# Inverse transforms in the FFN's PSUM ring next to forward ones, one place per step for convolution work, gated stores of kept spectra, and more heat matmuls

## The chip, the cores and the metric

The program runs on one core of one Trainium2 chip. The metric is the device time of one launch in microseconds, the median of several runs. Clocks: TensorE (PE) runs at one of two levels, 1.2 or 2.4 GHz; the profile gives the granted share, where 1.00 is 2.4 GHz and 0.50 is 1.2 GHz.

## What is computed

A long convolution, gated by x, is followed by a feed-forward network (FFN) on every token. Everything is float32 in and out.

```python
# x, v: [4, 12480, 128]; pos_emb: [12480, 64]; w_in: [128, 2048]; w_out: [2048, 128]
h_filt = (np.maximum(pos_emb @ w1, 0) @ w2) * np.exp(-0.01 * pos)[:, None]
y = irfft(rfft(x * v, 2 * S) * rfft(h_filt, 2 * S))[:, :S]
t = (x * y).reshape(49920, 128)
h = t @ w_in
out = (h * sigmoid(1.702 * h)) @ w_out
```

## The kernel before

The FFT is written as matmuls. A sequence half of 6240 points is split as 52 x 120, and the work is cut into five sets `o` (0 to 4): set 0 is the first half of batch 0 and of the filter, set 1 the first half of batch 1 and the filter's second half, set 2 the first halves of batches 2 and 3, sets 3 and 4 the second halves of all four. Each set passes three stages.

- **Stage p1** (`p1_start` for set 0, `p1_unit` for the others): transforms of 120 points, 26 units of a set; results go to DRAM (`g_d`).
- **Stage p2** (`p2_start` for set 0, `p2_unit` for the others): 31 units of a set. A unit loads its piece of `g_d`; `forward` (L315) makes the transform of 52 points, four float32 matmuls of 52 rows by 64 columns that sit on the four quarters of the array and write two PSUM banks; VectorE multiplies the spectra; `inverse` (L321), four matmuls of the same shape, goes back into two banks, which ScalarE copies out to `z`; a DMA writes `z_d`. In the trace each of these float32 matmuls is two records, so that a block of four is "x8".
- **Stage p3** (`p3_unit`): the last inverse step, sixteen records on L508, then the product with x, split into a high and a low part `xh`, `xl` for the FFN.

The FFN works on 104 "halves" of 480 tokens, eight steps each, 832 steps in all. A step is `mm1` (six matmuls of 480 columns into one of two tiles `h`, each two banks), two GELU passes on ScalarE (`fgh` rounded, `fg` full), one subtraction on VectorE (`fgl`, by `lo`), and three steps later `mm2` (six matmuls into `acc`). The first PSUM pool of this phase, tag `cv`, has three banks for all of the convolution; the tag `h` has two tiles of two banks; `acc` has one.

The order is by hand, in a fixed program order for each engine. At first set 0 passes p1 and p2 alone (the start phase), with `heat(k)`: 2k matmuls of zeros, 256 columns of bf16, whose results nobody reads. A short prologue computes `p3_unit(0)`. Then the 832 steps run, and the other sets' p1 and p2 units are fed in between: `feed.run(0.5)` stands at two places in a step, one after `mm1` and one after `mm2`, and lets as many pieces (up to a `yield`) of the units be written as the pace of that set asks for. `pipe` moves all live units on by one piece when a new one begins, so that a unit's inverse comes two units after its forward. All p2 units of sets 3 and 4 multiply two old spectra too (L410 to L424), so that they have more VectorE work.

24 of set 0's spectra are kept in SBUF until the FFN runs. They are stored by 48 DMAs that are written at steps 1 and 9 on GpSimd's queue (L706); the room that they leave is the later units' pool.

Names and lines that matter below: `forward` L318, `inverse` L324, `mm1` L581, `mm2` L598, GELU L582 and L583, `lo` L589, p3's matmuls L508, heat L655, the spectra's stores L375 and L376, p3's loads L482, L486 and L488, and the loads `pt` L193 and matmuls L198 with which set 1 begins.

## Time and profile before

| | us |
|---|---|
| median of 3 runs | 3064.37 (3063.86 to 3067.53) |
| the profiled execution | 3067.85 |
| its span, first to last instruction | 3066.1 |
| PE busy in the span | 3007.3 |
| VectorE (DVE) busy | 2153.9 |
| ScalarE (ACT) busy | 2068.8 |

The median is the number to beat; the profile is of one execution, whose span leaves out 1.75 us around the program. A busy PE is not a PE at its peak: matmuls overlap each other, their ends are modelled, and a record's length is longer than the distance to the next record. So the cost of a piece of PE work is read from the distance between starts, or from what a stretch holds beside a known number of steps.

### The profile page before, as it was taken

The page shows a single profiled execution, that of the slowest core. Times are in us where ns is not written, and L with a number is a line of the kernel's source. Part 1 is how long each engine was busy: PE and PEld are TensorE (multiplying, and loading weights), DVE is VectorE, ACT ScalarE, POOL GpSimd, SP SyncE. Part 2 cuts the span into 40 slices and gives each one's busy share as a digit, 9 for nine tenths or more (in the row PEclk, how much of TensorE's full clock was granted, in tenths as well). Part 3 has the DMA queues.
Part 4 walks back from the last instruction along what each step waited for, and adds up shares of the span by engine and source line. Part 5 has one row for each costly group of instructions (what it writes and reads, how often), then busy time and mean ns, then how long its engine had stood idle before and what let it go on. Part 6 is the DMA issues. An engine that isn't in the chain of part 4 may idle for free.

```text
span 3066.1 us, 42511 instructions
## 1 busy us (share of the span) xinstructions
PE 3007.3 (98%) x15368; PEld 2319.2 (76%) x15368; DVE 2153.9 (70%) x2909; ACT 2068.8 (67%) x2813; POOL 469.9 (15%) x764
## 2 busy tenths in 40 slices
PE   8889999999999999999999999999999999999999
PEld 4348876688666788777768887777778888888888
DVE  6656777777777667999996469898885444454444
ACT  3447766687777777666667766666667677767676
POOL 2363111022100111101111111011111111111110
PEclk9889999999999999999999999999999999999999
DMA  9889998899777966656665334454541111111110
GB/s 286 280 297 264 256 282 269 272 313 306 252 257 259 299 193 192 202 186 202 190 188 168 107 94 153 160 166 159 170 148 63 48 59 45 54 52 45 60 45 27
DMA packets 261105, 541.87 MB, mean 177 GB/s; under 512 B 30978, under 2 KB 120762, under 8 KB 260898
## 3 DMA queue, kind: packets, MB, share of 16 engines
q1 hardware_dynamic: 205970, 377.29, 39.0%
q0 software_dynamic: 54928, 161.86, 17.5%
q8 instruction: 124, 2.03, 0.3%
q14 instruction: 83, 0.68, 0.1%
HBM read 330.24 MB, written 208.80 MB: 176 GB/s over the span
## 4 chain that ended last, share of the span: by engine, by line
PE 63%; issue 27%; DVE 4%; POOL 3%; DMA 3%; ACT 1%; SPq 0%; POOLq 0%; ACTq 0%; DVEq 0%
PE acc L598 22%; PE h L581 22%; PE cv L318 4%; PE cv L508 4%; PE cv L324 4%; PE cv L178 1%; PE cv L179 1%; PE cv L180 1%; POOL zt L482 1%; PE cv L258 1%; DMA vt<-in_c_v_dram 1%; PE wb L655 1%; DVE fgl L589 1%; POOL out_dram L609 1%; POOL x L488 1%
## 5 line engine op out<-in xcount | busy, mean ns | idle before, releaser
L589 DVE TENSOR_TENSOR fgl<-fg,fgh 128x960 fp32r<-128x960 f32 x832 | 960.1, 1156 | 604.9 <-ACT fg L583 540.7
L582 ACT ACTIVATE fgh<-h 128x960 fp32r<-128x960 f32 x832 | 810.3, 974 | 574.3 <-PE h L581 573.6
L581 PE MATMUL h<-xh,wi 128*128 128x480 f32 x3328 | 1132.2, 384 | 1.3 <-ACT fg L583 1.2
L598 PE MATMUL acc<-fgh,wo 128*128 128x480 f32 x3328 | 884.2, 387 | 0.0
L583 ACT ACTIVATE fg<-h 128x960 f32<-128x960 f32 x832 | 807.3, 970 | 24.1 <-DVE fgl L589 24.0
L581 PEld LDWEIGHTS h<-xh,wi 128*128 128x128 f32 x3328 | 626.0, 188 | 188.7 <-issue 71.5
L598 PEld LDWEIGHTS acc<-fgh,wo 128*128 128x128 f32 x3328 | 610.2, 188 | 169.7 <-issue 81.7
L581 PE MATMUL h<-xl,wi 128*128 128x480 f32 x1664 | 632.2, 380 | 0.2 <-DVE xl L527 0.2
L598 PE MATMUL acc<-fgl,wo 128*128 128x480 f32 x1664 | 500.5, 382 | 1.7 <-DVE fgl L589 1.7
L609 POOL DMA_DIRECT2D out_dram<-ot x104 | 57.1, 549 | 2001.9 <-ACT ot L602 1999.9
L598 PEld LDWEIGHTS acc<-fgl,wo 128*128 128x128 f32 x1664 | 312.9, 188 | 51.5 <-DVE fgl L589 2.1
L581 PEld LDWEIGHTS h<-xl,wi 128*128 128x128 f32 x1664 | 312.8, 188 | 47.3 <-DVE xl L527 0.5
L508 PEld LDWEIGHTS cv<-vt,zt 122*128 122x128 f32 x1664 | 203.6, 194 | 29.1 <-issue 10.5
L508 PE MATMUL cv<-vt,zt 122*128 122x120 f32 x1664 | 206.6, 278 | 12.0 <-DMA vt<-in_c_v_dram 12.0
L318 PE MATMUL cv<-g,wf 52*64 52x512 f32 (+1 forms) x1240 | 186.0, 640 | 13.4 <-DVE t L355 5.7
L482 POOL DMA_DIRECT2D zt<-z_d x204 | 148.4, 733 | 14.9 <-issue 8.7
L466 ACT ACTIVATE z<-cv 128x512 f32<-128x512 f32 (+2 forms) x248 | 120.4, 544 | 43.0 <-PE cv L324 42.8
L324 PE MATMUL cv<-t,wv 52*64 52x512 f32 (+2 forms) x992 | 129.2, 555 | 5.4 <-DVE e L446 4.0
L311 ACT ACTIVATE a<-cv 128x512 f32<-128x512 f32 x208 | 119.0, 609 | 16.2 <-PE cv L180 15.3
L518 DVE TENSOR_TENSOR a<-cv,yq 128x240 f32<-128x240 f32 (+1 forms) x101 | 40.8, 404 | 119.8 <-ACT yq L516 119.6
L278 POOL DMA_DIRECT2D ft<-in_c_f_dram x108 | 57.6, 535 | 423.8 <-PE cv L180 420.1
L602 ACT ACTIVATE ot<-acc 128x480 f32<-128x480 f32 x104 | 59.5, 572 | 86.1 <-PE acc L598 86.1
(89 smaller groups left out, 2537.8 us busy)
## 6 DMA issues: line engine op xcount, KB each, us to landing
g_d<-a SPq DMA_DIRECT2D x260, 256.0 KB
g<-g_d SPq DMA_DIRECT2D x300, 208.0 KB
zt<-z_d POOLq DMA_DIRECT2D x204, 256.0 KB, 4.3
e<-e_d SPq DMA_DIRECT2D x180, 256.0 KB
z_d<-z SPq DMA_DIRECT2D x90, 512.0 KB
xt<-in_xv_dram SPq DMA_DIRECT2D x78, 480.0 KB
u<-us_d SPq DMA_DIRECT2D x60, 512.0 KB
ft<-in_c_f_dram POOLq DMA_DIRECT2D x108, 240.0 KB, 4.6
```

Of the source, the lines that this page charges most:

```text
L311: act(a[:, ri], b, ACTF.Copy)
L318: mm(out=xy[q ^ c][64 * c:64 * c + 64, 0:256 * nw].rearrange("p (w c) -> p w c", w=nw), lhsT=wf[64 * q:64 * q + N2, c], rhs=g[64 * q:64 * ...
L324: mm(out=ab[h][64 * pl:64 * pl + 64, 0:w].rearrange("p (w c) -> p w c", w=nw), lhsT=wv[64 * h:64 * h + N2, pl], rhs=y[pl ^ h][64 * h:64 * ...
L466: act(zv[:, :, h], ab[h][:, 0:wd].rearrange("p (w c) -> p w c", w=nw), ACTF.Copy)
L482: q.dma_start(out=zv[:, gq], in_=z_d[o][64 * gq + 2 * p0:64 * gq + 2 * p0 + 2 * npr].rearrange("r k c -> k r c"))
L508: mm(out=b[:, c0:c0 + M], lhsT=lhs, rhs=rhs, start=(k == 0), stop=(k == 1))
L581: mm(out=h[:, i, 0:TW], lhsT=wt[:, s], rhs=xx, start=st, stop=sp)
L582: act(gh, h[:, :, 0:TW], ACTF.Gelu_apprx_sigmoid)
L583: act(gf, h[:, :, 0:TW], ACTF.Gelu_apprx_sigmoid)
L589: tt(out=gl, in0=gf, in1=gh.bitcast(F32), op=ALU.subtract)
L598: mm(out=acc, lhsT=wt[:, 2 * k + i, :], rhs=xx[:, i], start=(t == 0 and i == 0 and k == 0), stop=(t == 2 and i == 1 and k == STEPS - 1))
L609: nc.gpsimd.dma_start(out=out[:, n], in_=ot)
```

## The change

The diff, in full:

```diff
--- before.py
+++ after.py
@@ -312,7 +312,13 @@
         yield
         g_out(j, p, a)
 
+    def behind():
+        go = shared.pop("inverse", None)
+        if go is not None:
+            go()
+
     def forward(g, nw, xy):
+        behind()
         for c in range(2):
             for q in range(2):
                 mm(out=xy[q ^ c][64 * c:64 * c + 64, 0:256 * nw].rearrange("p (w c) -> p w c", w=nw),
@@ -458,13 +464,19 @@
         tt(out=y[:, :, 1], in0=y[:, :, 1], in1=yb[:, :, 0], op=ALU.add)
         yield
         yield
-        _, ab = pair(False)
-        inverse([y[:, :, i] for i in range(2)], nw, wd, ab)
         z = sb("z", [128, 2, 2, 256], F32, 3, "az")
         zv = z.rearrange("p w a c -> p (w a c)")[:, 0:2 * wd].rearrange("p (w a c) -> p w a c", w=nw, a=2)
-        for h in range(2):
-            act(zv[:, :, h], ab[h][:, 0:wd].rearrange("p (w c) -> p w c", w=nw), ACTF.Copy)
-        yield
+
+        def back():
+            ab = ps["h"].tile([128, 2, 512], F32, tag="h", name="ab")
+            inverse([y[:, :, i] for i in range(2)], nw, wd, [ab[:, 0], ab[:, 1]])
+            act(zv.rearrange("p w a c -> p a w c"), ab[:, :, 0:wd].rearrange("p a (w c) -> p a w c", w=nw), ACTF.Copy)
+
+        behind()
+        shared["inverse"] = back
+        yield
+        if shared.get("inverse") is back:
+            behind()
         nc.sync.dma_start(out=z_d[j][:, 4 * v:4 * v + 2 * nw, :], in_=zv.rearrange("p w a c -> p (w a) c"))
 
     xts = {}
@@ -522,6 +534,8 @@
         yield
         if n0:
             tt(out=av[:, :, 0:n0], in0=av[:, :, 0:n0], in1=xw[:, :, 0:n0], op=ALU.mult)
+        shared["a3"] = a
+        yield
         act(xh, a, ACTF.Copy)
         yield
         tt(out=xl, in0=a, in1=xh.bitcast(F32), op=ALU.subtract)
@@ -666,7 +680,7 @@
                     p1_cm.__exit__(None, None, None)
                     ps["k"] = keep_cm.__enter__()
                 pipe.tick(u)
-                heat(1 if 4 < n < NP or n > NP + 9 else 2)
+                heat(1 if 4 < n < NP else 6 if NP < n < NP + 6 else 2)
                 if n == 4:
                     nc.sync.dma_start(out=wf, in_=c_wf)
                     nc.sync.dma_start(out=wv, in_=c_wi)
@@ -686,13 +700,15 @@
         begin = sorted(when(n) for n in first)
         feed = Feed(pipe, *conv_feed())
         feed.pace(0, begin[0] - HOLD)
-        for n in range(6):
+        for n in range(7):
             p3.tick(p3_unit(0) if n == 0 else None)
+            if n == 1:
+                act(sgn0, zero[:, 0:1], ACTF.Gelu_apprx_sigmoid)
             if n == 3:
-                act(sgn0, zero[:, 0:1], ACTF.Gelu_apprx_sigmoid)
                 b = bank()
                 for _ in range(20):
                     mm(out=b[:, 0:256], lhsT=warm[:, 0:128], rhs=warm, start=True, stop=True)
+        gate = shared["a3"]
         ffn = Ffn()
         pend = []
         for n in range(NH):
@@ -703,6 +719,8 @@
                     ffn.mm2(pend.pop(0))
                 pend.append(ffn.mm1(n, k))
                 t = n * STEPS + k
+                if t == 1:
+                    nc.gpsimd.tensor_tensor(out=sgn0, in0=gate[:, 0:1], in1=gate[:, 0:1], op=ALU.mult)
                 if t == 1 or t == 9:
                     for _ in range(KEEP // 2):
                         spec_store(*spectra.pop(0), nc.gpsimd)
@@ -711,8 +729,10 @@
                     for o in range(1, 5):
                         fill(o, nc.gpsimd)
                     ps["s"] = ctx.enter_context(tc.tile_pool(name="main", bufs=1, side="right", reuse_waits="tile"))
+                if len(pend) == LAG:
+                    ffn.mm2(pend.pop(0))
                 if t >= HOLD:
-                    feed.run(0.5)
+                    feed.run(1.0)
                 if n + 1 < NH:
                     new = None
                     if k == 0:
@@ -727,10 +747,6 @@
                     p3.tick(new)
                 if k == 4:
                     ffn.store()
-                if len(pend) == LAG:
-                    ffn.mm2(pend.pop(0))
-                if t >= HOLD:
-                    feed.run(0.5)
         ffn.lo(pend[-1])
         for it in pend:
             ffn.mm2(it)
```

In words:

- `p2_unit` no longer writes its inverse where it stands. It leaves it in `shared["inverse"]`, and the next `forward` writes it just ahead of its own four matmuls. Where no forward follows within a piece, the unit writes it itself.
- The inverse's two banks come from the FFN's ring (tag `h`) and no more from the three `cv` banks; one ScalarE copy takes both banks in place of two copies.
- In a step, `mm2` follows `mm1`, and all convolution work (`feed.run(1.0)`, then `p3.tick`) follows `mm2`.
- `p3_unit` has one more `yield`, between VectorE's product and ScalarE's copy to `xh`; the prologue has one more tick, and the GELU table is loaded two ticks earlier.
- GpSimd multiplies a column of the first half's `a3` into `sgn0` at step 1, ahead of the 24 stores written there. Nothing reads `sgn0`: the queue of stores waits until the first half has passed p3.
- Heat: 12 matmuls for 4 in the five rounds after the last p1 unit has begun (n = 27 to 31), and 4 for 2 in the 35 rounds from n = 36 on.

Three places show it in the order of the instructions. PE in set 2's p2 units, before: an inverse (L324) between `mm2` and `mm1`, and the forward (L318) that is next, sixteen rows later between `mm1` and `mm2`.

```order
L598 MATMUL acc<-fgh,wo_74 128x480 x2
L598 MATMUL acc<-fgl,wo_73 128x480 x2
L324 MATMUL cv<-t_12440,wv 64x512 x4
L581 MATMUL h<-xh,wi_71 128x480
L581 MATMUL h<-xl,wi_71 128x480
L581 MATMUL h<-xh,wi_72 128x480
```

```order
L581 MATMUL h<-xh,wi_72 128x480
L318 MATMUL cv<-g,wf 64x512 x4
L598 MATMUL acc<-fgh,wo_73 128x480 x2
L598 MATMUL acc<-fgh,wo_74 128x480 x2
L598 MATMUL acc<-fgl,wo_73 128x480 x2
```

The same place of PE in the changed kernel, whose lines are L612 for `mm2`, L330 for inverse, L324 for forward and L595 for `mm1`:

```order
L612 MATMUL acc<-fgh,wo_74 128x480 x2
L612 MATMUL acc<-fgl,wo_73 128x480 x2
L330 MATMUL ab<-t_12431,wv 64x512 x4
L324 MATMUL cv<-g,wf 64x512 x4
L595 MATMUL h<-xh,wi_71 128x480
L595 MATMUL h<-xl,wi_71 128x480
```

Inverse and forward now stand side by side, and the inverse's output is `ab`. In the FFN phase 114 of the 124 inverses have a forward right behind them; before there were 5 places where a forward and an inverse touched, the inverse behind.

GpSimd at the start of the FFN phase, before: the last two products of the start phase (L359, L360), then the stores of kept spectra (`eu`).

```order
L360 TENSOR_TENSOR y<-t_1788,t_1787 128x256
L359 TENSOR_TENSOR y<-t_1812,t_1813 128x128
L360 TENSOR_TENSOR y<-t_1813,t_1812 128x128
L375 DMA e_d<-eu 128x512
L376 DMA us_d<-eu 128x512
```

And in the changed kernel, where the same stores are L381 and L382:

```order
L366 TENSOR_TENSOR y<-t_1882,t_1881 128x256
L365 TENSOR_TENSOR y<-t_1908,t_1909 128x128
L366 TENSOR_TENSOR y<-t_1909,t_1908 128x128
L723 TENSOR_TENSOR sgn_65<-a_2071 128x1
L381 DMA e_d<-eu 128x512
L382 DMA us_d<-eu 128x512
```

The product L723, which reads the first half's `a3`, now stands ahead of every store of kept spectra.

## Rows read from the trace of the kernel before

**Rows 1.** The page's part 1: busy us (share of span) xinstructions.

```profile
PE 3007.3 (98%) x15368; PEld 2319.2 (76%) x15368; DVE 2153.9 (70%) x2909; ACT 2068.8 (67%) x2813; POOL 469.9 (15%) x764
```

**Rows 2.** Busy by stretch: us; PE, PEld, DVE, ACT, POOL busy; clock, DMA share, GB/s.

```profile
1200.00:1600.00 400.00, 396.56 (x2052) 286.91 (x2051) 395.91 (x534) 253.83 (x328) 44.41 (x73) 1.00 0.60 192
...
1850.00:2250.00 400.00, 400.00 (x2069) 304.37 (x2069) 354.88 (x420) 264.11 (x334) 45.79 (x75) 1.00 0.50 161
```

**Rows 3.** The same view of L582 alone (ACT, one instruction a step).

```profile
1300.00:1550.00 250.00, 68.40 (x71) 1.00 0.60 191
1850.00:2250.00 400.00, 117.24 (x121) 1.00 0.50 161
2400.00:3000.00 600.00, 205.69 (x212) 1.00 0.16 51
```

**Rows 4.** The same view of L324 alone (PE, PEld; eight records a block).

```profile
1300.00:1550.00 250.00, 20.69 (x152) 3.95 (x152) 1.00 0.60 191
1850.00:2250.00 400.00, 26.14 (x192) 4.99 (x192) 1.00 0.50 161
```

**Rows 5.** Timeline, PE and ACT: start us, us, instruction, [idle before <-releaser].

```profile
863.68 0.38 PE L581 MATMUL h<-xl,wi 128*128 128x480 f32 x1
...
863.90 0.38 PE L581 MATMUL h<-xh,wi 128*128 128x480 f32 x1
...
864.21 1.09 PE L318 MATMUL cv<-g,wf 52*64 52x512 f32 x8
...
864.32 0.97 ACT L582 ACTIVATE fgh<-h 128x960 fp32r<-128x960 f32 x1 [0.72 <-PE h L581]
...
865.12 1.02 PE L324 MATMUL cv<-t,wv 52*64 52x512 f32 x2
...
865.18 0.96 ACT L583 ACTIVATE fg<-h 128x960 f32<-128x960 f32 x1
...
866.69 1.08 PE L324 MATMUL cv<-t,wv 52*64 52x512 f32 x6 [0.55 <-ACT us L442]
```

**Rows 6.** Groups by line: out<-in xcount | busy us, mean ns | idle before <-releasers.

```profile
L508 PE MATMUL cv<-vt,zt 122*128 122x120 f32 x1664 | 206.6, 278 | 12.0 <-DMA vt<-in_c_v_dram 12.0
...
L324 PE MATMUL cv<-t,wv 52*64 52x512 f32 (+2 forms) x992 | 129.2, 555 | 5.4 <-DVE e L446 4.0 <-ACT us L442 1.1 <-ACT a L311 0.2
```

**Rows 7.** Waits of ScalarE: who <- on whom: us in total, times, longest.

```profile
ACT fgh L582 <- PE h L581: 573.6, 650, 3.3
...
ACT xh L525 <- DVE a L524: 51.3, 26, 5.0
```

**Rows 8.** Timeline from the start phase's end to set 1's first matmul.

```profile
195.65 0.71 POOL L375 DMA_DIRECT2D e_d<-eu  x1
...
196.23 8.91 PE L655 MATMUL wb<-zero 128*128 128x256 bf16 x80
...
203.15 1.67 SPq L486 DMA_DIRECT2D vt<-in_c_v_dram  x1
...
210.81 3.74 PE L508 MATMUL cv<-vt,zt 122*128 122x120 f32 x16 [5.68 <-DMA vt<-in_c_v_dram]
...
238.94 0.34 SPq L193 DMA_DIRECT2D pt<-in_posm_dram  x1
...
254.15 0.57 PE L198 MATMUL cv<-pt,w_sb 128*128 128x240 f32 x2
```

**Rows 9.** A later p3 block at full clock, same view.

```profile
247.11 1.94 PE L508 MATMUL cv<-vt,zt 122*128 122x120 f32 x16
```

**Rows 10.** Timeline of PE in the start phase, where p1 ends and p2 begins.

```profile
98.03 1.91 PE L655 MATMUL wb<-zero 128*128 128x256 bf16 x16
104.54 2.04 PE L318 MATMUL cv<-g,wf 52*64 52x512 f32 x5 [4.60 <-issue]
```

**Rows 11.** Busy by stretch in the start phase's p2 units, all engines.

```profile
130.00:140.00 10.00, 9.88 (x54) 2.69 (x54) 9.34 (x16) 5.27 (x10) 5.13 (x6) 0.50 0.92 316
150.00:160.00 10.00, 10.00 (x81) 3.42 (x81) 9.49 (x17) 7.17 (x15) 6.38 (x9) 1.00 0.89 313
```

## The prediction, made before the changed kernel was run

> **What bounds the kernel now.** I read the page's part 1 first: PE is busy 98% of the span [rows 1], so time can only come out of PE's own work, its waits, or the ends where it stands still. Which of these is worth what differs by stage, so the second view is the busy time by stretch. Set 3's p2 units run from 1200 to 1600 us, and there VectorE is busy 395.9 of 400 us: two engines are full, and VectorE has 4.1 us to spare. In set 4's stretch it is busy 354.9 of 400, and PE alone is full [rows 2]. Third, what a block of small matmuls costs PE. FFN alone makes 212 steps in 600 us, 2.83 us a step. Set 4's stretch has 121 steps in 400 us [rows 3], which by that take 342.4; 57.6 are left for 192/8 = 24 inverse blocks [rows 4] and as many forward ones, 1.20 us each. But where a forward is followed at once by an inverse, the second block starts 865.12 - 864.21 = 0.91 us after the first [rows 5]. So 0.29 us of every block that stands alone is the way into it and out of it: between the last `mm1` record and the block lie 0.31 us instead of the usual 0.22 [rows 5], and the rest is behind it.
>
> **The blocks side by side.** Before, 248 blocks stand in 243 runs (5 places touch); afterwards 114 inverses are followed by a forward, which makes 134 runs. That is 109 fewer: 25 in set 1, 26 in set 2, 29 each in sets 3 and 4. Sets 1, 2 and 4: 80 x 0.29 = **23.2 us**. In set 3 the same 29 x 0.29 = 8.4 us is not to be had, since VectorE keeps all its work and has 4.1 us of slack; in 250 us of it PE has 71 steps, 200.9 us, and 38 blocks at 1.29 us instead of 1.20 [rows 3, 4], so PE already waits there a little. Between 0 and 4.1 I take **2.5 us**. That two blocks with all their inputs ready follow each other without a gap is inferred: the row of 865.12 shows a start at 0.91 us, yet its second part waits.
>
> **The waits for `cv` banks.** At the five places where an inverse stands behind a forward, it starts with one matmul alone and waits for a bank that ScalarE or VectorE still reads: 866.69 - 865.12 = 1.57 us before the other three [rows 5]; L324's idle time, 5.4 us, names just these releasers [rows 6]. The inverse now takes its banks from `h`, and 5 x 1.57 = 7.9 us go. In its place comes a new wait. With an inverse in one `h` tile, the next `mm1` must take the tile of the `mm1` just before it, whose two GELUs end at 866.14, 1.9 us after its last record ends at 864.28 [rows 5]. In between lie `mm2`, 6 x 0.22 = 1.3 us, and the two blocks, 0.91 + 1.20 = 2.1 us: 1.5 us to spare. In the step at a half's end that has no `mm2`, one in eight, only 0.2 us are to spare. Nothing in the trace shows this wait; it costs 0 when ScalarE is on time, and 5 us if the 14 such pairs and some others lose 0.3 us. I take 2.4, as ScalarE stands idle before the GELU in 650 of 832 steps [rows 7]. Net **5.5 us**. The one worry in ScalarE's queue, its waits of 51.3/26 = 2.0 us for VectorE ahead of `xh` [rows 7], is what the new `yield` in p3 takes away; the product is then a step old. One copy for two banks saves ScalarE time that bounds nothing.
>
> A rule of the Trainium skill speaks against this part (Perfetto Trace Analysis, Optimizing Tensor Performance): independent groups should rotate through different PSUM banks, so that one is read while the next is written. By it the second `mm1` would wait for a reader each time; by the rows the reader is done 1.5 us earlier, and the sum stands as it is. The bad case is the first rival below.
>
> **The start of the FFN.** GpSimd's stores begin at 195.65, before the first half's loads (its `vt` at 203.15), and share the DMA queues with them; p3 waits for `vt` until 210.81, 5.68 us after the heat ended at 205.1 [rows 8]. With the stores behind the first half's p3 the loads run alone. PE cannot begin before the heat ends at 205.1; I put p3 at 205.8, 5 us earlier. It then runs its sixteen records in 1.94 us [rows 9] instead of 3.74 [rows 8], if the clock is still up. That is 6.8 us. Against it: the 48 stores now begin some 14 us later (p3 at 205.8, and 3.9 us to the product), and set 1's `pt` waits for room that they leave. Before, it was issued at 238.94 and used at 254.15 [rows 8], 15.2 us apart. It moves back by something between 0 and 14 us, since the loads that shared the queues with the first stores are through by then; at 8 us, and used 7 us earlier, the 15.2 us are just used up. Between 0 and 6.8 I take **5.5 us**. Other work that waits behind the gate on GpSimd's queue are the loads of the third half; they have some ten steps.
>
> **p3 behind `mm2`.** Two later waits for `vt` make up the other 12.0 - 5.7 = 6.3 us of L508's idle time [rows 6]. p3 now stands after the step's `mm2`, 6 x 0.22 = 1.3 us later, which hides so much of each: **2 us** (0 to 2.6).
>
> **Heat.** A heat matmul takes 8.91/80 = 0.111 us [rows 8]. Of the 40 added at p1's end, 24 fall into the 4.6 us in which PE waits for `g` [rows 10]; 16 stand ahead of the last p1 blocks, on the path: +1.8 us. The 70 others are 7.8 us at full clock. They cost nothing where p2 waits for VectorE, busy 9.49 of 10 us at full clock, and at most these 7.8. The gain: at half clock PE gets 54 records done in 10 us, at full clock 81 [rows 11]. But VectorE is busy 9.34 of 10 us in the half-clock row too, so what a full clock gives is a few us at most. I take **+1 us** (from -4 to +6).
>
> Here rule and row part. The Trainium skill (TensorE: Matmul & The Clock Gate, Part 1) says that the throttled clock is the default and that activity releases it; PE is busy 9.88 of 10 us in the first of these rows and the clock stays at 0.50. By the rule more heat would save up to a third of such a stretch, 3 us in those 10; by the row it is not sure to raise the clock at all, and the sum above goes by the row.
>
> **The sum.** 23.2 + 2.5 + 5.5 + 5.5 + 2 - 1 = 37.7 us. On the profiled execution that is a span of 3066.1 - 37.7 = 3028.4 and about 3030 with the 1.75 us around it; that execution lies 3.5 us above the median of 3064.37, from which the same sum gives 3026.7, so **3027 us**.
>
> **Rivals.** (1) *The ring of `h` becomes the bound, and the kernel slower.* Place: the `mm1` behind each of the 114 pairs. It decides from the point where ScalarE ends its GELUs more than 1.5 + 37.7/114 = 1.8 us late at every pair; at 2.0 us late it costs 114 x 0.5 = 57 us and gives 3084. For it: ScalarE has other copies in its queue, and the wait has no slack in one step of eight. Against it: it waits for PE in 650 steps of 832 [rows 7]. Chance 0.07. (2) *The change does not do what it says*: blocks stand side by side but the array still empties between an inverse and a forward, or the forward waits for `cv` banks. Then only 5.5 + 5.5 + 2 - 1 = 12 us remain: 3052. For it: no pair in the trace ran through without a wait [rows 5]. Against it: with the inverse gone from `cv`, forwards have three banks for two. Chance 0.1. (3) *Late data at the start*: set 1's loads come later than reckoned, and the start gives back its gain and some: 0 instead of 5.5, and heat at its full +6, hence 37.7 - 5.5 - 5 = 27 us, 3037. Chance 0.13. The forecast, within 3010 to 3036, has 0.66; the rest of the chance, 0.04, is for no change, where new waits eat all.
>
> **Range and chances.** The low end adds the best bounds: 23.2 + 4.1 + 7.9 + 6.8 + 2.6 + 4 = 48.6, and a few us for the price of a block, which I know to 10%: 3012. The high end keeps 23.2 alone and heat at +6: 3047. A measurement of this kernel can tell some 6 us (0.2%) from no change. Faster: 0.66 + 0.1 + 0.13 = 0.89; within 0.2%: 0.04; slower: 0.07.
>
> **What would show it.** In the changed profile: forward blocks that start 0.9 us after their inverse, and set 4's 400 us holding 24 pairs in 24 x 2.1 = 50.6 instead of 57.6 us; set 3's stretch hardly shorter, with VectorE full; L324's idle time for `e` and `us` gone; the first p3 block near 205 to 206 us at full clock; no large idle time of PE in front of `mm1` with GELU as its releaser, which would be rival 1. Wrong would be a set-4 stretch as long as before (rival 2), or idle PE at the first `pt` matmuls (rival 3).

## The result: slower, and the profile after

The changed kernel takes **3091.66 us** (median of 4 runs, 3088.13 to 3093.0) against 3065.79 us for the kernel before, run beside it (3063.86 to 3067.53): a ratio of 1.0083, with an interval of 1.0065 to 1.010. It is 26 us slower where 3027 us, 38 faster, was forecast, and it lies outside the range of 3012 to 3047 us. The profiled execution has a span of 3091.2 us. One execution of all those below, the fourth of e8, ran at a granted clock of 0.555 (4904 us) and is left out of e8's time.

The first line of the page's part 1 after the change, engine by engine, beside [rows 1]:

```profile
PE 2991.3 (97%) x15478; PEld 2351.4 (76%) x15478; DVE 2150.2 (70%) x2909; ACT 2085.6 (67%) x2689; POOL 470.6 (15%) x765
```

PE is still the busiest engine, but it now stands still far more. The waits of PE after the change (engine, tile and line, what it waited for: us in total, times, longest):

```profile
PE h L595 <- DVE xl L541: 36.3, 29, 3.2
...
PE cv L198 <- DMA pt<-in_posm_dram: 10.9, 2, 7.7
PE h L595 <- ACT fg L597: 8.4, 14, 1.6
...
PE cv L520 <- DMA vt<-in_c_v_dram: 5.5, 4, 3.8
...
PE ab L330 <- ACT fg L597: 0.6, 1, 0.6
```

L595 is `mm1`, L541 the subtraction that makes `xl`, L198 the matmul on `pt`, L330 the inverse, L324 the forward (L581, L528, L198, L324 and L318 before). The waits for `cv` banks that the inverse had before in this phase [rows 6] are gone, and the one that rival 1 feared, `mm1` behind GELU, is 8.4 us. The large new one is `mm1` waiting for VectorE's `xl` at the start of a half, 29 times. From the first p3 block to the end, PE's gaps of 0.15 us and more sum to 68 us, against 23 before.

The same stretches of the program, found by the start of GELU number 26, 104 and 208, then set 4's. Windows after the change, then of before (stretch, its length; busy us and records of PE, PEld, VectorE, ScalarE, GpSimd; granted clock; DMA share; GB/s):

```profile
323.90:666.40 342.50, 333.22 (x1826) 250.65 (x1825) 251.79 (x444) 245.76 (x380) 46.91 (x80) 1.00 0.92 278
666.40:1106.50 440.10, 420.87 (x2181) 316.61 (x2180) 317.27 (x423) 327.80 (x449) 63.12 (x107) 0.98 0.85 266
1690.00:2400.00 710.00, 700.25 (x3619) 565.44 (x3618) 550.91 (x648) 478.58 (x567) 86.04 (x142) 1.00 0.42 136
```

```profile
313.80:658.60 344.80, 340.76 (x1826) 248.95 (x1824) 252.05 (x441) 242.30 (x411) 46.90 (x80) 1.00 0.92 275
658.60:1090.90 432.30, 424.89 (x2187) 310.39 (x2186) 322.26 (x427) 327.06 (x483) 63.65 (x108) 1.00 0.88 272
1665.00:2375.00 710.00, 708.26 (x3624) 560.74 (x3623) 551.62 (x649) 477.31 (x598) 86.03 (x141) 1.00 0.42 136
```

For the same number of PE records (to within 6), PE's busy time falls by 7.5 us in set 1's stretch, 4.0 in set 2's, and 8.0 in set 4's. The pairs do save PE's time. The stretches hardly get shorter by it: set 1's loses 2.3 us, set 4's 8.0 us less work is followed by 8 us more idle, and set 2's stretch is longer than before.

The timelines of the start, after the change (us from the span's start, duration, engine, line, operation). First p3 and the stores:

```profile
196.33 9.78 PE L669 MATMUL wb<-zero 128*128 128x256 bf16 x88
205.95 1.94 PE L520 MATMUL cv<-vt,zt 122*128 122x120 f32 x16
...
210.44 0.71 POOL L381 DMA_DIRECT2D e_d<-eu  x1 [0.30 <-issue]
```

```profile
248.08 0.34 SPq L193 DMA_DIRECT2D pt<-in_posm_dram  x1
251.09 1.75 SPq L193 DMA_DIRECT2D pt<-in_posm_dram  x1
252.16 1.17 PE L198 MATMUL cv<-pt,w_sb 128*128 128x240 f32 x2 [3.17 <-DMA pt<-in_posm_dram]
...
269.37 1.17 PE L198 MATMUL cv<-pt,w_sb 128*128 128x240 f32 x2 [7.71 <-DMA pt<-in_posm_dram]
```

p3 starts at 205.95 in 1.94 us, as forecast. Then the bill: the stores start at 210.44 instead of 195.65 [rows 8], the first `pt` load is issued at 248.08 instead of 238.94, and PE waits 3.17 and 7.71 us for `pt`.

### The profile page after: what moved, and what is told of

Read it like the earlier page. It is cut to its first block, busy times and chain, and to the rows that moved or that the text cites. A ratio compares the mean times of both kernels' runs of the same rounds, so it can differ in the third digit from the quotient of the medians.

```text
span 3091.2 us, 42465 instructions
## 1 busy us (share of the span) xinstructions
PE 2991.3 (97%) x15478; PEld 2351.4 (76%) x15478; DVE 2150.2 (70%) x2909; ACT 2085.6 (67%) x2689; POOL 470.6 (15%) x765
## 4 chain that ended last, share of the span: by engine, by line
issue 38%; PE 17%; DVE 7%; POOL 4%; DMA 1%; ACT 0%; SPq 0%; POOLq 0%; DVEq 0%
PE h L595 7%; PE acc L612 7%; DVE fgl L603 2%; POOL zt L494 2%; DVE t L423 1%; PE cv L520 1%; POOL out_dram L623 1%; POOL x L500 1%; DVE t L439 1%; DVE t L438 1%; POOL vt L498 1%; DVE t L443 1%; PE ab L330 1%; DVE t L441 1%; PE cv L178 1%
## 5 line engine op out<-in xcount | busy, mean ns | idle before, releaser
L595 PE MATMUL h<-xh,wi 128*128 128x480 f32 x3328 | 1143.7, 388 | 9.2 <-ACT fg L597 8.4
L612 PE MATMUL acc<-fgh,wo 128*128 128x480 f32 x3328 | 871.9, 384 | 0.0
L595 PEld LDWEIGHTS h<-xh,wi 128*128 128x128 f32 x3328 | 630.5, 189 | 184.7 <-issue 38.1
L612 PEld LDWEIGHTS acc<-fgh,wo 128*128 128x128 f32 x3328 | 629.6, 190 | 111.6 <-issue 12.2
L595 PE MATMUL h<-xl,wi 128*128 128x480 f32 x1664 | 638.2, 384 | 36.3 <-DVE xl L541 36.3
L612 PE MATMUL acc<-fgl,wo 128*128 128x480 f32 x1664 | 503.2, 384 | 0.5 <-DVE fgl L603 0.4
L595 PEld LDWEIGHTS h<-xl,wi 128*128 128x128 f32 x1664 | 315.0, 189 | 91.7 <-DVE xl L541 47.2
L612 PEld LDWEIGHTS acc<-fgl,wo 128*128 128x128 f32 x1664 | 314.8, 189 | 51.7 <-DVE fgl L603 1.3
L520 PEld LDWEIGHTS cv<-vt,zt 122*128 122x128 f32 x1664 | 200.4, 192 | 26.2 <-issue 10.1
L324 PE MATMUL cv<-g,wf 52*64 52x512 f32 (+1 forms) x1240 | 174.4, 606 | 13.3 <-DMA g<-g_d 7.3
L473 ACT ACTIVATE z<-ab 128x1024 f32<-128x1024 f32 (+2 forms) x124 | 112.6, 908 | 33.8 <-PE ab L330 28.6
L311 ACT ACTIVATE a<-cv 128x512 f32<-128x512 f32 x208 | 121.0, 602 | 17.3 <-PE cv L180 11.7
L459 DVE TENSOR_TENSOR t<-us,e 128x512 f32<-128x512 f32 (+2 forms) x62 | 58.5, 943 | 100.3 <-PE ab L330 55.6
L278 POOL DMA_DIRECT2D ft<-in_c_f_dram x108 | 57.5, 534 | 450.2 <-PE cv L180 436.4
L330 PE MATMUL ab<-t,wv 52*64 52x512 f32 (+2 forms) x992 | 120.3, 555 | 0.8 <-ACT fg L597 0.6
```

Of the source, the lines that this page charges most:

```text
L311: act(a[:, ri], b, ACTF.Copy)
L324: mm(out=xy[q ^ c][64 * c:64 * c + 64, 0:256 * nw].rearrange("p (w c) -> p w c", w=nw), lhsT=wf[64 * q:64 * q + N2, c], rhs=g[64 * q:64 * ...
L330: mm(out=ab[h][64 * pl:64 * pl + 64, 0:w].rearrange("p (w c) -> p w c", w=nw), lhsT=wv[64 * h:64 * h + N2, pl], rhs=y[pl ^ h][64 * h:64 * ...
L473: act(zv.rearrange("p w a c -> p a w c"), ab[:, :, 0:wd].rearrange("p a (w c) -> p a w c", w=nw), ACTF.Copy)
L520: mm(out=b[:, c0:c0 + M], lhsT=lhs, rhs=rhs, start=(k == 0), stop=(k == 1))
L595: mm(out=h[:, i, 0:TW], lhsT=wt[:, s], rhs=xx, start=st, stop=sp)
```

## The experiments

Times are medians; "before" in each is the kernel before, run beside it (3065 to 3066 us in every group). Two theories stood at first. A: the added `yield` in p3 makes `xl` late. B: VectorE's queue is late, and the wait only moves when the `yield` goes. Beside them C: the gate delays `pt`.

### The added step in p3, and the gate

Without the step (changed kernel; the first p3 then has six ticks, not seven):

```diff
         shared["a3"] = a
-        yield
         act(xh, a, ACTF.Copy)
```

> The changed kernel without the added step in p3: the cast to `xh` stands in the same step as the product again, and `xl` one step earlier; everything else as changed. Theory A (the added step makes `xl` late, and the 36.3 us in which mm1 waits for it, with the stretches at half clock behind such waits, some 10 us, are its price): 3092 - 36 - 10 = 3046 us, between 3038 and 3054, PE's wait at L595-like mm1 for `xl` under 5 us in all. Theory B (VectorE's queue is late by 4 to 5 us in the p2 stages because all convolution work now stands in one place, so the wait only moves, to ScalarE's GELU or to `xl` one step later): 3080 to 3092, and the idle time in front of mm1 stays above 25 us.

Measured: **3111.4 us** (1.0145, 1.013 to 1.016), 20 us slower still and outside both ranges. Theory A has fallen. The waits of PE and of ScalarE in this run:

```profile
PE h L594 <- ACT fg L596: 42.9, 28, 4.5
...
PE ab L330 <- ACT fg L596: 10.3, 8, 2.2
```

```profile
ACT xh L538 <- DVE a L536: 123.3, 41, 6.2
```

ScalarE now stands 123.3 us at the cast to `xh`, waiting for VectorE's product, with the GELUs behind it in its queue, and `mm1` waits for GELU instead of for `xl`. The wait moved and grew: the step had been a remedy for a late VectorE, not the disease.

Without the gate (changed kernel):

```diff
-                if t == 1:
-                    nc.gpsimd.tensor_tensor(out=sgn0, in0=gate[:, 0:1], in1=gate[:, 0:1], op=ALU.mult)
```

> The changed kernel without the product on GpSimd ahead of the stores of the kept spectra; the stores are issued at the same place of the program and wait for nothing. Theory C (the gate makes the stores late, these keep the first `pt` loads of set 1 waiting; 10.9 us of PE's idle time and some 6 us of half clock behind it are its price, and the start's 6.6 us gain falls back by about 5): 3092 - 17 + 5 = 3080 us, between 3074 and 3084; the wait for `pt` under 2 us. Rival D (the `pt` loads wait for something else, such as room in the pools or their place on SP's queue): 3092 to 3097, the waits of 3.2 and 7.7 us for `pt` stay within 2 us of that.

Measured: **3087.0 us** (1.0062, 1.0045 to 1.0079), 4.7 less than with it where 12 less was expected, so above theory C's range. The waits for `pt` are gone, as theory C has it, and the start's gain with them:

```profile
PE h L595 <- DVE xl L541: 36.5, 29, 3.2
PE cv L520 <- DMA vt<-in_c_v_dram: 15.7, 4, 8.9
```

From the first GELU to the 26th the run takes 94.4 us, as before (94.4), instead of 111.2; at that point it is 11 us ahead of the changed kernel, of which 4.7 are left at the end. The `xl` waits do not depend on the gate.

Without both:

> The changed kernel without the added step in p3 and without the gate. Theories A and C together: 3046 - 12 = 3034 us, between 3024 and 3042, faster than the kernel before by 25 to 40 us, which is what the blocks side by side and the `cv` waits were to bring. By theory B it stays over 3070.

Measured: **3105.1 us** (1.0124): e1 less 6 us for the gate. This rested on theory A and missed with it.

The kernel before with the step alone:

```diff
+        yield
         act(xh, a, ACTF.Copy)
         yield
         tt(out=xl, in0=a, in1=xh.bitcast(F32), op=ALU.subtract)
```

> The kernel before with the added step in p3 alone. If the step is enough by itself to make `xl` late: 29 or more waits of about 1.2 us, 3066 + 36 = 3100 us. If it takes the late VectorE queue of the changed kernel as well (in the kernel before the queue is about 1 us late in the p2 stages, against 4 to 5): within 4 us of 3066, and less than 4 us of mm1's waiting for `xl`.

Measured: **3064.5 us** (0.9993, 0.9983 to 1.0004). The step alone does nothing measurable; `mm1` waits 4.8 us for `xl` in it, where under 4 was expected.

The kernel before with step and gate:

> The kernel before with the gate on the kept spectra (and the added step in p3, which alone gave 3064.5 us, since the gate reads the first product). If the gate costs what it seemed to cost in the changed kernel (the start 6 us earlier, then 16.8 us lost at the first `pt` loads): 3064.5 - 6 + 17 = 3075 us, between 3069 and 3079, PE's wait for `pt` some 11 us. If the loads of `pt` were late there through the other edits: 3058 to 3061, no wait for `pt`.

Measured: **3072.4 us** (1.0019, 1.001 to 1.0028), 8 us over e4. The start (the view ends at 200 us, after nine of p3's sixteen records) and the wait:

```profile
198.99 1.23 PE L508 MATMUL cv<-vt,zt 122*128 122x120 f32 x9
```

```profile
PE cv L198 <- DMA pt<-in_posm_dram: 12.3, 2, 7.1
```

The first GELU starts 12.3 us earlier than in e4, and 26 GELUs later the run is 4.7 us behind it. The gate loses more at `pt` than it wins at the start, in either kernel.

### One place, or pairs?

What makes VectorE late? The lag, from the end of the second GELU to VectorE's `lo` (a mean over some 26 steps in the p2 units), went from 1.5 to 4.3 us in set 1 and from 0.9 to 4.9 in set 2. By theory F the one place of the conv work makes it, by theory P the pairs do. Four kernels without the gate vary the order of a step or leave the pairs out. Two places again:

```diff
                 pend.append(ffn.mm1(n, k))
...
-                if len(pend) == LAG:
-                    ffn.mm2(pend.pop(0))
                 if t >= HOLD:
-                    feed.run(1.0)
+                    feed.run(0.5)
...
                     ffn.store()
+                if len(pend) == LAG:
+                    ffn.mm2(pend.pop(0))
+                if t >= HOLD:
+                    feed.run(0.5)
```

> The changed kernel without the gate, with the convolution's work at two places of a step again (half of it ahead of p3's part and `mm2`, half behind), inverses still deferred to the next forward. Theory F (the lateness of VectorE comes from the one place: all of a step's conv work stands in its queue ahead of p3's product and `xl` and of the next `lo`): the lag of `lo` falls back from 4 to 5 us to 1 to 2 us in the p2 stages of sets 1 and 2, mm1 waits for `xl` under 8 us instead of 36, and the time is 3087 - 28 - 10 = 3049 us, between 3040 and 3058, faster than before. Theory P (it comes from the pairs: forward and inverse back to back hand ScalarE and VectorE their work in one burst): lag and waits stay, 3078 to 3090.

p3 first, one place:

```diff
-                if len(pend) == LAG:
-                    ffn.mm2(pend.pop(0))
-                if t >= HOLD:
-                    feed.run(1.0)
                 if n + 1 < NH:
...
                     p3.tick(new)
+                if len(pend) == LAG:
+                    ffn.mm2(pend.pop(0))
+                if t >= HOLD:
+                    feed.run(1.0)
```

> The changed kernel without the gate, with p3's part of a step ahead of `mm2` and of the conv work, which stays at one place. Theory F: product, `xh` and `xl` then stand ahead of the conv work of their own step, 2 to 3 us of VectorE time; the waits for `xl` fall from 36 us to under 10, while the lag of `lo` stays at 4 to 5 us; 3087 - 27 - 8 + 2 (p3 is behind `mm2` no more) = 3054 us, between 3046 and 3066. Theory P: the queue in front of `xl` is that of the step before anyhow, and 3080 to 3090.

The whole of p3 a step earlier:

```diff
         xts[n] = xh, xl
         yield
         yield
-        yield
```

> The changed kernel without the gate, with the whole of p3 one step earlier (two steps instead of three between its loads and its matmuls), so that `xl` stands where it stood before the change and the cast to `xh` is still a step behind the product. If the lateness of `xl` at the start of a half is all that the lag of VectorE costs: the 36 us and some 10 us of half clock go, and the waits for `vt` grow by up to 10: 3087 - 46 + 5 = 3046 us, between 3036 and 3056. If the lag costs elsewhere as soon as this wait is gone (GELU and `h` banks): 3065 to 3085.

No pairs, one place:

```diff
-        def back():
-            ab = ps["h"].tile([128, 2, 512], F32, tag="h", name="ab")
...
-        behind()
-        shared["inverse"] = back
+        _, ab = pair(False)
+        inverse([y[:, :, i] for i in range(2)], nw, wd, ab)
+        for h in range(2):
+            act(zv[:, :, h], ab[h][:, 0:wd].rearrange("p (w c) -> p w c", w=nw), ACTF.Copy)
```

> The changed kernel without the gate and without the pairs: the inverse runs at once in two `cv` banks as before, still at one place of a step. Theory F: lag of 4 us and waits for `xl` of 30 to 40 us remain and the gain of the pairs is gone: 3087 + 25 = 3112 us, between 3100 and 3122. Theory P: the lag falls to 1 to 2 us, the waits for `xl` below 8 us, 3066 us give or take 8.

| | time, us | ratio | wait for `xl` | for GELU at `mm1` | for `vt` | lag in set 2 (GELU 156 to 181) |
|---|---|---|---|---|---|---|
| before | 3065.4 | 1 | 0.2 | 1.2 | 12.0 | 0.9 |
| e2, no gate | 3087.0 | 1.0062 | 36.5 | 9.0 | 15.7 | 4.9 |
| e5, two places | 3059.3 | 0.9983 | 10.1 | 11.8 | 14.0 | 4.2 |
| e6, p3 first | 3063.0 | 0.999 | 11.2 | 12.9 | 14.3 | 4.8 |
| e7, p3 a step earlier | 3083.5 | 1.0057 | 2.3 | 13.8 | 32.8 | 4.8 |
| e8, no pairs | 3090.5 | 1.0085 | 15.3 | 0.8 | 13.5 | 1.5 |

Two things come apart. **The order** of the step costs time: e5 and e6, which put p3's VectorE work ahead of half or all of the conv work, gain 24 to 28 us over e2, as theory F had it (e5 within 2 us of its range, e6 inside it). **The lag** follows the pairs: it is 1.5 us without them and over 4 with them, whatever the order, as theory P had it. The time of e8 lies outside both ranges. With e4 (two places, no pairs, 3064.5; it has the heat of before, the others the added one) the four corners read: two places 3064.5 without and 3059.3 with pairs; one place 3090.5 and 3087.0. One place costs 26.0 or 27.7 us, and the pairs gain 5.2 or 3.5, where 26 and the `cv` waits were forecast. e7 cures `xl` and pays with `vt`: the loads have a step less. In e8 the waits for `xl` (4.8 us in e4, 15.3) and for `cv` banks that VectorE reads for `e` (4.0 and 10.7) grow by 17.2 us of its 26; the rest of the price of one place without pairs stays open.

e5 also shows where the pairs' gain stays away. By GELU numbers, set 4's stretch (364 to 572) takes 667.2 us against 675.0 in e4: 7.9 us, as forecast. But sets 1 and 2 (26 to 104, 104 to 208) gain 2.2 and lose 1.0, where 7 each and the `cv` waits were due (what was expected of e10, below, takes set 2's loss for a gain of 1.1).

### The buffer behind the lag

What differs between set 4 and sets 1 and 2 stands in the timeline. After the change, in set 2, PE and VectorE only (in brackets: idle time before, and its releaser):

```profile
886.12 1.09 PE L330 MATMUL ab<-t,wv 52*64 52x512 f32 x8
887.03 1.04 PE L324 MATMUL cv<-g,wf 52*64 52x512 f32 x8
887.34 1.23 DVE L459 TENSOR_TENSOR t<-us,e 128x1024 f32<-128x1024 f32 x1 [0.41 <-issue]
...
888.48 1.22 DVE L461 TENSOR_TENSOR t<-us,e 128x1024 f32<-128x1024 f32 x1
...
889.61 1.15 DVE L603 TENSOR_TENSOR fgl<-fg,fgh 128x960 fp32r<-128x960 f32 x1
...
890.68 0.68 DVE L463 TENSOR_TENSOR t<-t,t 128x512 f32<-128x512 f32 x1
...
891.28 0.68 DVE L464 TENSOR_TENSOR t<-t,t 128x512 f32<-128x512 f32 x1
891.89 0.65 DVE L541 TENSOR_TENSOR xl<-a,xh 128x480 fp32r<-128x480 f32 x1
...
892.59 0.48 PE L595 MATMUL h<-xl,wi 128*128 128x480 f32 x1 [1.23 <-DVE xl L541]
...
895.19 1.09 PE L330 MATMUL ab<-t,wv 52*64 52x512 f32 x8
```

Then a GELU of ScalarE, and the next product:

```profile
894.84 0.97 ACT L597 ACTIVATE fg<-h 128x960 f32<-128x960 f32 x1
...
896.40 1.23 DVE L459 TENSOR_TENSOR t<-us,e 128x1024 f32<-128x1024 f32 x1 [2.80 <-ACT fg L597]
```

VectorE's first product of a unit (L459) starts 0.13 and 0.12 us after the inverse ends: 887.21 and 887.34, 896.28 and 896.40. In the second case VectorE stood 2.80 us for it. The view names GELU as the releaser, but that had ended at 895.81, 0.59 us ahead, and the product reads nothing of it; the inverse ended last. The reason that the program offers is a buffer. The product is written to `t1`, which has two buffers, and `t1` is also the `y` that the inverse of the unit two before reads. Before the change that inverse stood in the program at its own unit's turn, ahead of this product. Now it waits until the next `forward` pops it, which in a tick of sets 1 and 2 comes after the younger unit's product. So VectorE waits, in order, until PE has come past `mm2` to the deferred inverse, with `lo`, the p3 products and `xl` in its queue behind the wait. In sets 3 and 4 the product comes behind the same unit's forward, in front of which the inverse runs; there it costs nothing.

The first product's line between 800 and 1050 us, in before, changed kernel and e5 (busy us, mean ns; idle time before and its releasers):

```profile
L453 DVE TENSOR_TENSOR t<-us,e 128x1024 f32<-128x1024 f32 (+1 forms) x28 | 33.7, 1202 | 12.3 <-ACT fgh L582 6.5 <-PE cv L324 4.9 <-issue 0.9
```

```profile
L459 DVE TENSOR_TENSOR t<-us,e 128x1024 f32<-128x1024 f32 (+1 forms) x29 | 35.0, 1206 | 60.4 <-ACT fg L597 29.7 <-PE ab L330 15.9 <-DMA xt<-in_xv_dram 7.6
```

```profile
L459 DVE TENSOR_TENSOR t<-us,e 128x1024 f32<-128x1024 f32 (+1 forms) x28 | 33.8, 1206 | 43.6 <-ACT fgh L596 19.1 <-PE ab L330 15.3 <-ACT fg L597 7.0
```

This theory (T) has a cheap test: a third buffer. The tile `t3`, which only sets 3 and 4 use, takes every third unit of sets 1 and 2:

```diff
-        t1, y = tmp("t1", 2)
+        third = not blk and v % 3 == 2
+        t1, y = tmp("t3" if third else "t1", 1 if third else 2)
```

On e2 (one place), on e5 (two places) and on e6 (p3 first):

> The changed kernel without the gate, and with a third buffer in turn for the first product of a p2 unit in sets 1 and 2 (the tile `t1`, which is also the `y` that the inverse reads; the third is the tile `t3`, idle in these sets). Theory T (the deferred inverse reads `y` a step's part later, the product two units on needs that buffer, so VectorE waits in order for PE, 60.4 us of idle time at L459 between 800 and 1050 us against 12.3 before, and everything behind it is late): that idle time falls below 20 us, the lag of `lo` in sets 1 and 2 from 4 to 5 us to about 2, the waits for `xl` from 36 us to some 15, and the time from 3087 to about 3055 us, between 3044 and 3066. Theory P (the burst of work that a pair hands to ScalarE and VectorE makes the lag, whatever the buffers): 3080 to 3090.

> The same third buffer with the convolution's work at two places of a step. Two places alone gave 3059 us; there sets 1 and 2 gained 2.2 and 1.1 us from the pairs, where 25 and 26 pairs at 0.29 us and the `cv` waits (4.0 and 1.1 us) were to bring 11.3 and 8.6. Theory T: they now gain it: 3059 - 9 - 7.5 = 3043 us, between 3036 and 3050, clearly faster than before. Theory P: 3055 to 3062.

> The same third buffer with one place per step and p3's part ahead of it. Without the buffer that gave 3063 us. Theory T: 3063 - 14 = 3049 us, between 3042 and 3056. Theory P: 3059 to 3067.

Measured: e9 **3047.1 us** (0.9942, 0.9927 to 0.9957), e10 **3039.1 us** (0.9918, 0.9903 to 0.9933), e11 **3033.8 us** (0.990, 0.9884 to 0.9917): 40, 20 and 29 us less than without the buffer. e9 and e10 lie in theory T's ranges, e11 beyond its on the fast side. Theory P is out. The product's line over the same 250 us in e2, then in e9:

```profile
L459 DVE TENSOR_TENSOR t<-us,e 128x1024 f32<-128x1024 f32 (+1 forms) x28 | 33.8, 1206 | 57.5 <-ACT fg L597 36.9 <-PE ab L330 13.8 <-ACT fgh L596 5.1
```

```profile
L460 DVE TENSOR_TENSOR t<-us,e 128x1024 f32<-128x1024 f32 (+1 forms) x26 | 31.2, 1202 | 10.5 <-ACT us L449 10.5
```

Its idle time is back from 57.5 us in e2 (60.4 in the changed kernel) to 10.5, and the lag in set 2 from 4.9 to 1.05 us. The waits of PE in e9 and in e11:

```profile
PE h L596 <- DVE xl L542: 24.9, 19, 3.2
...
PE h L596 <- ACT fg L598: 5.2, 10, 0.9
```

```profile
PE cv L521 <- DMA vt<-in_c_v_dram: 14.9, 4, 8.7
...
PE h L596 <- DVE xl L542: 9.0, 6, 2.5
PE h L596 <- ACT fg L598: 6.1, 9, 1.5
```

The buffer takes away 11.6 us of the 36.5 of `xl` waits with one place, which leaves 24.9 where some 15 were expected; most of that goes with the order. These waits are not all of the gain. Between the profiled executions of e2 and e9 PE's idle time falls by 21.6 us and its busy time by 17.3 (2985.9 to 2968.6). Of the busy time an estimated 7 us are the clock's: the stretches at 0.50 shrink from 30.7 us in all to 17.1, and half of the difference is lost time. The other 10 us are not explained.

### What is whose

Four more runs, to part the buffer's own worth, the step and the heat. The changed kernel with the buffer alone:

> The changed kernel as it is, gate and order included, with nothing but the third buffer for the first product in sets 1 and 2. Theory T: without the gate the buffer brought 3087 to 3047 us; the gate cost 4.7 us there, so 3052 us, between 3046 and 3058, faster than before by one buffer alone. If what the buffer brings depends on the start of set 1 that the gate delays: above 3060.

Measured: **3056.6 us** (0.9971, 0.9961 to 0.9981). One buffer turns the change from 26 us slower to 9 us faster, gate and order kept; PE's wait for `pt` is still 13.6 us there.

The kernel before with the buffer alone:

> The kernel before with the third buffer alone. Theory T (before the change the inverse had read the buffer in time, so that it lacked nothing): 3065 us, between 3061 and 3068. If the buffer is worth something by itself, and the 30 us of the best kernel so far are not the pairs': below 3055.

Measured: **3064.8 us** (0.9999, 0.9989 to 1.0008). Without the deferred inverse the buffer is worth nothing by itself: the gain of e10, and most of that of e11, comes with the deferred inverses. Whether it is their place next to a forward, their banks in `h` or the single copy, no run parts.

e11 without the step in p3:

> The kernel with p3 first, the third buffer and no gate (3033.8 us), without the added step in p3. If the step was worth 20 us in the changed kernel only because VectorE was late there and the cast to `xh` held ScalarE's queue up behind the product: now within 5 us of 3034. If the cast waits for the product at any lag: 3044 to 3054, with GELU waited for by mm1 for over 15 us.

Measured: **3032.3 us** (0.9891, 0.9875 to 0.9908), not to be told from e11. ScalarE waits 45.0 us, 27 times, for the product (123.3 us in e1). With VectorE on time the step is worth nothing, which closes the question of e1.

e11 with the heat of before:

```diff
-                heat(1 if 4 < n < NP else 6 if NP < n < NP + 6 else 2)
+                heat(1 if 4 < n < NP or n > NP + 9 else 2)
```

> The same kernel (3033.8 us) with the heat of the kernel before. The prediction put the added heat at 1 us of loss, between a gain of 4 and a loss of 6: 3033 us, between 3028 and 3038. If the added heat shortens the start by more, over 3040.

Measured: **3028.9 us** (0.9881, 0.9865 to 0.9896), the best kernel here: 37 us faster than before and 63 faster than the changed kernel. It is 4.9 us below e11, but the two did not run in one group and their intervals overlap. Their profiled runs differ mostly in when `vt` lands for the first p3:

```profile
209.50 3.74 PE L521 MATMUL cv<-vt,zt 122*128 122x120 f32 x16 [8.68 <-DMA vt<-in_c_v_dram]
```

```profile
205.37 3.74 PE L521 MATMUL cv<-vt,zt 122*128 122x120 f32 x16 [5.64 <-DMA vt<-in_c_v_dram]
```

e11 is the first, e16 the second: 4.1 us. Kernels with the same heat differ as much there, so the heat's price stays somewhere between 0 and 5 us.

The stages, by the starts of GELU numbers, in us:

| from GELU to GELU | before | changed | e5 | e9 | e10 | e11 |
|---|---|---|---|---|---|---|
| 0 starts at | 219.3 | 212.7 | 218.0 | 217.3 | 222.4 | 218.0 |
| 0 to 26 (first `pt` loads) | 94.4 | 111.2 | 94.2 | 94.4 | 94.3 | 94.8 |
| 26 to 104 (set 1) | 344.8 | 342.4 | 342.6 | 331.2 | 331.0 | 335.1 |
| 104 to 208 (set 2) | 432.3 | 440.1 | 434.6 | 420.1 | 423.0 | 418.0 |
| 208 to 364 (set 3) | 553.6 | 561.5 | 551.4 | 558.7 | 551.5 | 552.5 |
| 364 to 572 (set 4) | 674.8 | 676.4 | 667.2 | 677.6 | 667.2 | 666.1 |

The buffer acts in sets 1 and 2 (e5 to e10: -11.6 and -11.6), the order in sets 3 and 4 (e9 to e11: -6.2 and -11.5), where the buffer has no part. Each column is one execution. The kernels without pairs at two places (before, e4, e12, e14) agree within 0.3 us in set 4 and within 1.6 in set 1, but take 432.3 to 436.4 us in set 2. In set 3 those with the step in p3 (e4, e12) take 550.4, the others 553.6.

## Why the prediction was wrong, step by step

**Blocks side by side (23.2 + 2.5 us): the price was about right, the path was not.** With the third buffer and two places (e10), set 4 gains 7.6 us where 29 x 0.29 = 8.4 were reckoned, and sets 1 and 2 together 23.1, where 14.8 and the `cv` waits' 5.5 were. Set 3 is 2.1 us shorter than before (2.5 reckoned), but not shorter than in e4, which has the step in p3 as e10 has (550.4): there PE's busy time falls by 8.4 us and the length does not, as the text had it of a stage that VectorE fills. The pairs run through without a wait between their blocks, which the text had left as inferred. In e11, set 4:

```profile
1828.63 1.09 PE L330 MATMUL ab<-t,wv 52*64 52x512 f32 x8
1829.54 1.04 PE L324 MATMUL cv<-g,wf 52*64 52x512 f32 x8
1830.51 0.48 PE L596 MATMUL h<-xh,wi 128*128 128x480 f32 x1
```

The second block starts 0.91 us after the first, as [rows 5] had it, and `mm1` follows at 1.88 us. The failing step is what the text did not ask: it costed the inverse's move on PE and on ScalarE's copy, and followed its output (the `h` ring), but not its input. A reader that is moved back holds its input's buffer longer. That one omission is worth 40 us (e2 to e9), 35 with the gate in place (e13) and 20 with two places (e5 to e10).

**p3 behind `mm2` (2 us): the wrong sign.** The term took the 1.3 us that `mm2` hides of a `vt` wait, and did not count that p3's VectorE work moved too, behind a whole step's conv work in VectorE's queue, with `mm1` of the next half waiting for its last piece. p3 first gains 24 us without the third buffer (e2 to e6) and 13 with it (e9 to e11). [rows 7] showed ScalarE's waits for exactly these products; the text read them as ScalarE's affair.

**The step in p3 (costed at nothing): right, for the wrong reason.** Alone it does nothing (e4), and with VectorE on time neither (e15). In the changed kernel it is worth 20 us (e1), as a remedy. That `xl` came a step nearer to its use was not weighed at all; this became the place where the lateness was seen.

**`cv` waits (5.5 us): half held.** The waits of the inverse for `e` and `us` are gone. What was to take their place came out larger: for GELU `mm1` waits 8.4 us in the changed kernel and 6.1 in e11, where 1.2 of before and 2.4 were reckoned, and in e10 `mm1` waits 4.5 and the inverse 7.8. The net gain of this term alone no run shows.

**The start (5.5 us): its gain was there, its price under-reckoned.** p3 began at 205.95 (205.8 forecast) in 1.94 us, and the FFN 6.6 us earlier. "At 8 us, and used 7 us earlier, the 15.2 us are just used up" put the move at 8; it was 9.1 (248.08 for 238.94). The larger wait was not looked at. The second `pt` load took 19 us from its issue to its use before, with nothing to spare (the weight load of that matmul waited 0.29 us for it):

```profile
242.62 1.60 SPq L193 DMA_DIRECT2D pt<-in_posm_dram  x1
...
261.98 0.67 PE L198 MATMUL cv<-pt,w_sb 128*128 128x240 f32 x2
```

It takes 18 after the change; issued at 251.09, it holds PE for 7.71 us at 269.37. PE's clock falls at the two waits. (The text has stores and loads share the DMA queues; by their sums GpSimd's transfers are the page's q0 and SyncE's its q1, and what they share is the 16 DMA engines, busy 0.91 of the time in both windows.) From 240 to 290 us, after and before:

```profile
240.00:290.00 50.00, 39.13 (x161) 32.63 (x160) 22.78 (x39) 25.71 (x37) 17.03 (x28) 0.83 0.91 264
```

```profile
240.00:290.00 50.00, 50.00 (x244) 42.95 (x243) 31.91 (x55) 36.12 (x54) 10.90 (x18) 1.00 0.91 248
```

39.13 us busy instead of 50.00, at a mean granted clock of 0.83: 161 records instead of 244. The stage 0 to 26 loses 16.8 us for a start 6.6 us earlier.

**Heat (1 us): inside its bounds**, between 0 and 5 us of loss.

**The rivals.** Rival 1, the ring of `h`, did not decide; 8.4 us of waits, not 57. Rival 2 did not happen, although its sign, a stretch of set 4 as long as before (676.4 for 674.8 us), did: the order of the step made it, and it goes with p3 first (666.1 in e11). Rival 3, late data at the start, happened, and worse than its zero. The slower side came from two mechanisms that were not on the list: a buffer, and the order in VectorE's queue. From the changed kernel to e16 the steps are the gate 4.7 us (e2), the buffer 39.9 (e9), p3 first 13.3 (e11) and the heat 4.9 (e16), which the runs do not tell from nothing: 62.8 in all. That e16 lies 37 us below the kernel before, as the sum of 37.7 had it, is chance: it has neither the gate nor p3 behind `mm2` nor the added heat, 6.5 us of the sum, and sets 1 and 2 gained more than was reckoned.

## What to carry to other kernels

When an instruction is deferred, cost its inputs as well as its output: list who next writes each buffer that it reads, on which engine, and what stands behind that write in its in-order queue. A wait shown at one place (`mm1` for `xl`) may be only where lateness is seen; ask what the late engine itself waited for, and distrust a named releaser that had already ended when something else did. Work that the next stage waits for goes ahead of bulk work in every queue it passes, not only in the one that the edit is about.

## What the runs showed of the hardware that was not expected

A few us of idle PE cost more than themselves. In the changed kernel the granted clock falls to half at six of the eight longest waits for `xl` (2.0 to 3.2 us). Around the one that ends at 1852 us:

```profile
1846.00:1852.00 6.00, 2.76 (x16) 1.20 (x15) 5.97 (x8) 1.95 (x2) 0.00 (x0) 1.00 0.72 227
1852.00:1856.00 4.00, 4.00 (x11) 3.40 (x12) 4.00 (x6) 1.73 (x2) 0.00 (x0) 0.57 0.02 7
```

After 6 us in which PE was busy 2.76, the next 4 us run at a mean of 0.57, most of them at 0.50, the lower of the two levels (1.2 of 2.4 GHz), with PE busy throughout and 11 records done; in the 4 us behind them, at 1.00, it does 20. Between the first GELU and the last, the clock is at 0.50 in 11 stretches of the changed kernel (47.8 us in all), in 2 before (6.8 us), and in 3 in e11 (10.2 us). The other five of the 11 stand at two waits for `pt` and one each for `g`, `vt` and GELU; two waits for `xl` of 2.0 and 2.1 us, at 1246 and 1624 us, bring none. The Trainium skill (TensorE: Matmul & The Clock Gate, Part 1) says that the throttled clock is the default and that activity releases it; these rows agree in that the clock is down behind a pause and up again while PE is busy. In the start phase the rows don't agree so plainly: from 90 to 195 us the mean granted clock is 0.80 in the kernel before and 0.93 in e16, with the same heat.

The price of a pair was the other surprise: in set 1's stretch PE's busy time falls from 340.76 us before to 326.74 us in e9 for 1826 and 1825 records, 14.0 us for 25 pairs, while set 4's shows 8.0 us for 29. Part of the 14.0 is not the pairs': before has a stretch at 0.50 there, from 601.0 us, and e9 none, which is an estimated 1.7 us; and three inverse blocks of before stop inside for a `cv` bank, at 425, 562 and 599 us, of which an estimated 1.9 us count as busy. Why the other 10 us or so are still more for a pair than set 4's, although set 1's inverse is half as wide, stays open.
